# Segment loop of a recurrent-memory attention: smaller working tiles, 46 instead of 44 weight blocks resident in SBUF

## The chip, the cores and the metric

The kernel runs on one core of one Trainium2 chip. The metric is the device time of one execution in microseconds; of repeated executions the median counts. The engines are TensorE (PE in the profile), VectorE (DVE), ScalarE (ACT), GpSimd (POOL) and SyncE (SP); sixteen DMA engines move data between HBM and SBUF.

## What is computed

Two independent parts are computed and concatenated along the last axis. Part A is an attention with 32 heads of 128 over segments of 32 rows, with 8 memory rows that come from the segment before:

```python
mem = mem0                                  # 8 x 1024
for s in range(64):                         # 2048 rows in segments of 32
    h = concatenate([mem, x[32*s : 32*s+32]])        # 40 rows
    q, k, v = h @ Wq, h @ Wk, h @ Wv                 # 1024 -> 32 heads x 128 each
    p = softmax(where(mask, q @ k.T / sqrt(128), -1e9))
    o = (p @ v) @ Wo                                 # 4096 -> 1024
    mem = o[:8]                                      # into the next segment
    out_a[32*s : 32*s+32] = o[8:]
```

Since the memory of a segment is the output of the one before, the 64 segments run one after the other. The four weights have 4 million bf16 elements each, 32 MB together, which is more than SBUF holds. Part B is a state-space convolution of a 2048 x 1024 input with 128 complex modes per channel, done as a discrete Fourier transform with matmuls; the change does not touch it.

## The kernel before

**Order of the whole.** First part B is computed; in its shadow, on the same queues, everything of part A that doesn't depend on the memory is prepared (class `Ahead`, L60): the transposed x of each segment (`XTd`), and for the last 8 rows of each segment, which the code calls left rows, their projections k, q and v, packed as 768 columns per segment (`PKd`). Then comes the segment loop (L273 to L454), which is the subject here, and at the end an epilogue that projects the left rows' outputs of all segments with Wo at once (L458 on), from `OLd`. Inside the loop a segment therefore has 32 "main" rows in the projections: 24 rows of x and 8 memory rows. They sit in `hT`, [128, 8 chunks of 1024, 32 rows].

**Weights.** The weights are cut into 64 blocks of 128 x 2048 bf16 (512 KB, 4 KB per partition): for k, q and v each 2 halves t (16 heads) of 8 chunks kc of the contraction, and 16 units of Wo (two heads each). 44 blocks stay in SBUF for the whole loop (`W_res`). 20 are streamed in every segment from a DRAM copy: `STREAM` (L24) names the chunks kc of each projection and `STREAM_O` (L25) the units of Wo. `unit` (L223) returns the resident tile or issues a load on SP's queue into one of the four slots of `wst`. A load waits until the matmuls that use the slot's former block are done. The loop is written under a manual schedule: each engine executes its instructions in the order in which the code issues them, and waits come from data and from slots that are reused.

**A segment.** `quads` (L278) multiplies hT with the eight chunks of one half of a projection: per chunk four matmuls, 32 columns of the array each, that run beside each other, into one PSUM bank `acc`. `evac` copies it to SBUF as bf16 on ACT. `tr` (L295) transposes the 16 heads with TensorE into a PSUM tile, copied on DVE to KT or on ACT to QT. `scores` (L308) sets the mask with a matmul and adds q k^T for the main rows (index 0) and for the left rows (index 1), whose q is read from `pk`, into a PSUM tile `sc` of 8 x 40 columns. The keys are 32 main and 8 left ones. `softmax_a` (L321) takes the maximum, subtracts it in PSUM (DVE) and writes the exponential to an SBUF tile `ex` in bf16 (ACT). `softmax_b` (L329) sums and scales `ex` on DVE. `ptrans` (L336) transposes its 32 x 32 blocks on DVE into `pt` (main keys) and `pl` (left keys). `blocks` (L343) spreads them, multiplied by constant masks, to block-diagonal operands: `pb` and `lb` for the main queries on DVE, `pbl` and `lbl` for the left queries on POOL (`left_blocks`, L372). `pv` (L347) multiplies them with V. `oproj` (L378) multiplies the result oT with Wo, per unit eight matmuls, again four beside each other, into `po`.

The order in time is: k0, q0, k1, scores and softmax of half 0, q1, v0, scores and softmax of half 1, v1 (with pv of half 0 in its middle), projection units 0 to 7, pv of half 1, both pv of the left rows into `pvl`, units 8 to 15, then `osb` (L441), its transposition back into hT (`tro`, L448 and L449) and the stores. On POOL's queue lie the small loads and stores: `load_xt` one segment ahead, the copy into hT (`put_xt`), `load_pk`, the store of the left rows' oTL to `OLd` (L451) and four stores of osb (L454). `WARM` and `TAIL` are 0, so `warm` issues nothing; its PSUM tile still takes a bank.

PSUM's eight banks are divided in two for `acc`, two for `tr`, two for `att` (sc, pv, pvl), one for `warm` and one for `po`.

Of the kernel before, what the change touches and what calls it, by code (L numbers as in the profile page):

```python
# [23 lines left out]
STREAM = {("k", 0): (0, 4), ("q", 0): (0, 4), ("k", 1): (0, 4), ("q", 1): (0, 4), ("v", 0): (0, 4), ("v", 1): (0, 3, 6)}  # L24
STREAM_O = (0, 2, 5, 7, 9, 12, 14)  # L25
# [34 lines left out]
class Ahead:  # L60
# [34 lines left out]
    def projections(self, ps, tag):  # L95
# [11 lines left out]
        n = 0  # L107
        for i, (m, t, c) in enumerate(slices):
            w = ws[i]
            g, h2 = c // 2, 2 * (c % 2)  # L110
            mo = 0 if m == "k" else 256
            if m != "v" and c == 0:
                st = self.pool.tile([128, NS, 4, 4, XL], BF16, name="kst", tag="kst")
            for j in range(2):
# [26 lines left out]
                elif c == 7 and j == 1:  # L141
                    for r in range(8):
                        def put(r=r, mo=mo, t=t, st=st):
                            nc.sync.dma_start(out=PKd[8 * r:8 * r + 8, :, mo + 128 * t:mo + 128 * t + 128].rearrange("s p f -> p s f"),
                                              in_=st[:, 8 * r:8 * r + 8].rearrange("p s a b c -> p s (a b c)"))
                        late.append(put)
# [29 lines left out]
def part_a(ctx, tc, x, mem0, src, WD, HE, seg_len, out_a, ahead, W_res, rest):  # L176
# [12 lines left out]
    WARM = 0  # L189
    TAIL = 0  # L190
# [53 lines left out]
    ps_w = ctx_l.enter_context(tc.tile_pool(name="a_warm", bufs=1, space=PSUM))  # L244
    warm_ps = ps_w.tile([128, 512], F32, name="warm")
    warm_w = W_res["k", 0, 1]

    def warm(n):

        for _ in range(n):  # L250
            nc.tensor.matmul(warm_ps[:], lhsT=ident[:], rhs=warm_w[:, 0:512], start=True, stop=True, skip_group_check=True)
# [19 lines left out]
    xt = load_xt(1)  # L271
    pk = load_pk(0)
    for s in range(NS):  # L273
        vl = pk[:, 512:768].rearrange("p (t e) -> p t e", t=2)
        kl = pk[:, 0:256].rearrange("p (t a g k) -> p t a g k", t=2, a=4, g=4)
        ql = pk[:, 256:512].rearrange("p (t a g k) -> p t a g k", t=2, a=4, g=4)

        def quads(m, t, kcs, a=None):  # L278
            if a is None:
                a = ps_acc.tile([128, 512], F32, name="acc", tag="acc")  # L280
            for kc in kcs:
                w = unit((m, t, kc))
                if (m, t, kc) not in W_res:
                    warm(WARM)
# [18 lines left out]
        def new_kt(t):  # L303
            k = work.tile([128, 4, 4, NK], BF16, name="KT", tag="KT%d" % t)
            nc.gpsimd.tensor_copy(out=k[:, :, :, SL:NK], in_=kl[:, t])
            return k

        def scores(t, QT, KT):  # L308
# [6 lines left out]
            for hl in range(4):  # L315
                for g in range(4):
                    nc.tensor.matmul(sc[32 * g:32 * g + XL, 1, hl, :], lhsT=ql[:, t, hl, g, :], rhs=KT[:, hl, g, :],  # L317
                                     start=False, stop=True, tile_position=(0, 32 * g), skip_group_check=True)
            return sc[:].rearrange("p a b k -> p (a b) k")

        def softmax_a(sc):  # L321
# [3 lines left out]
            ex = work.tile([128, 8, NK], BF16, name="ex", tag="ex")  # L325
            nc.scalar.activation(out=ex[:], in_=sc, func=ACT.Exp, scale=scale)
            return ex

        def softmax_b(ex):  # L329
            ss = work.tile([128, 8], F32, name="ss", tag="ss")  # L330
            nc.vector.tensor_reduce(out=ss[:], in_=ex[:], axis=AX.X, op=ALU.add)
            rs = work.tile([128, 8], F32, name="rs", tag="rs")
            nc.vector.reciprocal(out=rs[:], in_=ss[:])
            nc.vector.tensor_tensor(out=ex[:], in0=ex[:], in1=bc(rs[:].unsqueeze(2), [128, 8, NK]), op=ALU.mult)

        def ptrans(t, ex):  # L336
            pt = work.tile([128, 8, 32], BF16, name="pt", tag="pt", bufs=2)
            nc.vector.transpose(out=pt[:], in_=ex[:, :, 0:SL])  # L338
            pl = work.tile([128, 2, 32], BF16, name="pl", tag="pl", bufs=2)
            nc.vector.transpose(out=pl[:], in_=ex[:, :, SL:NK])  # L340
            return pt, pl

        def blocks(eng, pt, pl, n, pb, lb):  # L343
            eng.tensor_tensor(out=pb, in0=bc(pt.unsqueeze(2), [128, 4, 4, n]), in1=bc(BD[:].unsqueeze(1).unsqueeze(3), [128, 4, 4, n]), op=ALU.mult)  # L344
            eng.tensor_tensor(out=lb, in0=bc(pl.unsqueeze(1), [128, 16, n]), in1=bc(BDL[:].rearrange("p a b -> p (a b)").unsqueeze(2), [128, 16, n]), op=ALU.mult)  # L345

        def pv(p, t, V, pb, lb):  # L347
            for hl in range(4):
                nc.tensor.matmul(p[:, hl, :], lhsT=V[:, 128 * hl:128 * hl + 128], rhs=pb[:, hl, :, :].rearrange("p a b -> p (a b)"),  # L349
                                 start=(hl == 0), stop=False, skip_group_check=True)  # L350
            nc.tensor.matmul(p.rearrange("p a b -> p (a b)"), lhsT=vl[:, t, :], rhs=lb.rearrange("p a b -> p (a b)"),  # L351
                             start=False, stop=True, skip_group_check=True)

        def new_qt(t):
            return work.tile([128, 4, 4, SL], BF16, name="QT", tag="QT%d" % t)

        def soft_blocks(t, ex):
            softmax_b(ex)
            pt, pl = ptrans(t, ex)
            pb = work.tile([128, 4, 4, SL], BF16, name="pb", tag="QT%d" % t)  # L360
            lb = work.tile([128, 16, SL], BF16, name="lb", tag="KT%d" % t)
# [789 lines left out]
```

## Time and profile before

| | |
|---|---|
| time, median of 3 runs | 3127.32 us (3118.98 to 3138.32) |
| the profiled execution's own time, its span | 3130.83 us, 3129.1 us |
| busy: PE, PEld, DVE, ACT, POOL | 70%, 36%, 42%, 31%, 25% of the span |
| HBM read, written | 809.26 MB, 68.42 MB |
| mean granted TensorE clock | 0.884 |
| share of SP's queue in the time of 16 DMA engines | 72.3% |

How to read it: the share of busy time is an average over part B (the first third), the loop (two thirds) and the epilogue, so the loop has to be looked at by itself. A busy TensorE is not TensorE at its peak, since the ends of matmuls are modelled. "Idle before" in a group of instructions is the time in which the engine waited, and the name behind it is what came last; idle time of an engine that is not the bound costs nothing. Times without unit in profile lines are us, durations of one instruction ns.

### The profile page before, as it was taken

What the parts mean: (1) busy time and instruction counts of PE and PEld (TensorE: products, weight loads), DVE (VectorE), ACT (ScalarE), POOL (GpSimd) and SP (SyncE); (2) the same over time, 40 slices, a digit from 0 to 9 for tenths busy, and PEclk for the clock granted to TensorE, in tenths of its full rate; (3) what the DMA queues carried; (4) which work ended last, traced back from release to release, by engine and by line L of the source; (5) the groups of instructions that cost most, each with busy time, mean ns of one, the idle gap of its engine ahead of it and who ended that gap; (6) DMA issues with size and microseconds to landing.
All of it is one profiled execution on the core that took longest, in us unless ns stands there. A gap on an engine that the chain in (4) does not pass through costs nothing.

```text
span 3129.1 us, 75740 instructions
## 1 busy us (share of the span) xinstructions
PE 2197.9 (70%) x32774; PEld 1139.2 (36%) x32774; DVE 1301.2 (42%) x2302; ACT 968.3 (31%) x1394; POOL 772.8 (25%) x1249
## 2 busy tenths in 40 slices
PE   1487778756975777777777777777677777777747
PEld 0255445522432333333333333333333333333323
DVE  7576777749851323232323232323332232323220
ACT  4776888611211222222222222212222222222210
POOL 2344344340001222222222222222222122222210
PEclk7699999868987898999998988889998899989878
DMA  4456653453358999999999999999999999999991
GB/s 119 134 156 187 189 150 104 126 159 104 122 198 314 352 348 351 349 350 351 352 342 337 351 344 348 333 346 332 347 356 341 331 353 345 342 355 346 347 330 56
DMA packets 394655, 868.02 MB, mean 277 GB/s; under 512 B 116726, under 2 KB 187382, under 8 KB 392272
## 3 DMA queue, kind: packets, MB, share of 16 engines
q1 hardware_dynamic: 353634, 789.62, 72.3%
q0 software_dynamic: 24912, 51.52, 5.0%
q10 hardware_dynamic: 15774, 22.03, 2.2%
q8 instruction: 256, 4.19, 0.5%
q14 instruction: 79, 0.65, 0.1%
HBM read 809.26 MB, written 68.42 MB: 280 GB/s over the span
## 4 chain that ended last, share of the span: by engine, by line
DMA 52%; PE 21%; issue 13%; ACT 5%; DVE 4%; POOL 4%; SPq 1%; ACTq 0%; POOLq 0%; DVEq 0%
DMA wst<-WD_o 17%; DMA wst<-WD_q 15%; DMA wst<-WD_v 11%; PE acc L286 8%; DMA wst<-WD_k 5%; PE po L386 4%; PE pe L480 2%; DMA olr<-OLd 1%; ACT sn L863 1%; PE pro L125 1%; POOL us L747 1%; POOL us L748 1%; PE pv L349 1%; DMA PVd<-vst 1%; PE ups L742 1%
## 5 line engine op out<-in xcount | busy, mean ns | idle before, releaser
L286 PEld LDWEIGHTS <-hT 128*32 128x32 bf16 x12288 | 317.1, 99 | 646.5 <-issue 338.4
L286 PE MATMUL acc<-wst,hT 128*32 128x512 bf16 x3328 | 348.9, 405 | 279.7 <-DMA wst<-WD_k 113.7
L292 ACT CAST qk<-acc 128x512 bf16<-128x512 f32 x256 | 149.8, 585 | 763.0 <-PE acc L286 762.0
L386 PEld LDWEIGHTS <-oT 128*32 128x32 bf16 x8192 | 243.1, 109 | 375.6 <-issue 303.2
L386 PE MATMUL po<-wst,oT 128*32 128x256 bf16 x3584 | 213.3, 321 | 236.9 <-DMA wst<-WD_o 234.1
L344 POOL TENSOR_TENSOR pbl<-pt,BD 128x128 bf16<-128x128 bf16 x128 | 91.3, 713 | 822.4 <-DVE pt L338 818.1
L298 DVE COPY KT<-tr 128x512 bf16<-128x512 bf16 x128 | 54.4, 425 | 569.9 <-PE tr L297 569.9
L441 DVE CAST osb<-po 128x256 bf16<-128x256 f32 x64 | 27.2, 425 | 584.6 <-PE po L386 584.6
L386 PE MATMUL po<-W_o,oT 128*32 128x256 bf16 x4608 | 250.0, 318 | 22.4 <-ACT oT L369 22.4
L286 PE MATMUL acc<-W_q,hT 128*32 128x512 bf16 x3072 | 231.2, 406 | 0.0
L286 PE MATMUL acc<-W_k,hT 128*32 128x512 bf16 x3072 | 231.1, 408 | 0.0
L286 PE MATMUL acc<-W_v,hT 128*32 128x512 bf16 x2816 | 211.3, 383 | 0.0
L369 ACT CAST oT<-pv 128x512 bf16<-128x512 f32 x128 | 74.8, 585 | 435.7 <-PE pv L351 435.7
L454 POOL DMA_DIRECT2D out_dram<-osb x256 | 129.2, 512 | 198.6 <-DVE osb L441 187.8
L1037 PE MATMUL yp<-Bt,mi 128*128 128x512 bf16 x384 | 116.8, 413 | 34.7 <-DVE Bt L991 17.1
L323 DVE TENSOR_REDUCE mx<-sc 128x8 f32<-128x320 f32 x128 | 62.3, 487 | 187.3 <-PE sc L317 187.2
L955 PE MATMUL hps<-KT,MF 128*128 128x512 bf16 x384 | 100.2, 410 | 51.9 <-DVE x L966 29.0
L298 ACT COPY QT<-tr 128x512 bf16<-128x512 bf16 x128 | 74.9, 585 | 151.9 <-PE tr L297 145.6
L125 PE MATMUL pro<-xTl,wsl 128*128 128x512 bf16 x512 | 115.1, 380 | 7.6 <-DVE ua L744 4.6
L345 DVE TENSOR_TENSOR lb<-pl,BDL 128x512 bf16<-128x512 bf16 x128 | 119.4, 933 | 0.0
L256 POOL DMA_DIRECT2D pk<-PKd x64 | 37.5, 586 | 325.1 <-PE pvl L351 316.5
L839 DVE SCALAR_TENSOR_TENSOR nr<-kM,ptt 128x656 f32<-128x656 f32 x128 | 106.1, 829 | 20.6 <-ACT kM L838 20.5
(259 smaller groups left out, 3876.8 us busy)
## 6 DMA issues: line engine op xcount, KB each, us to landing
wst<-WD_o SPq DMA_DIRECT2D x448, 512.0 KB, 5.7
wst<-WD_v SPq DMA_DIRECT2D x320, 512.0 KB, 5.4
wst<-WD_k SPq DMA_DIRECT2D x256, 512.0 KB, 5.6
wst<-WD_q SPq DMA_DIRECT2D x256, 512.0 KB
Ud<-ux POOLq DMA_DIRECT2D x16, 1024.0 KB, 5.5
uq<-Ud SPq DMA_DIRECT2D x32, 512.0 KB, 5.1
pk<-PKd POOLq DMA_DIRECT2D x64, 192.0 KB, 5.3
wsl<-in_A_Wk_dram SPq DMA_DIRECT2D x16, 512.0 KB, 5.4
```

Source lines behind the costliest of these rows:

```text
L125: nc.tensor.matmul(a[:], lhsT=w[:, kc, 128 * j:128 * j + 128], rhs=xTl[:, kc, :, :].rearrange("p s k -> p (s k)"), start=(kc == 0), stop=( ...
L286: nc.tensor.matmul(a[32 * g:32 * g + 32, :], lhsT=hT[:, kc, :], rhs=w[:, 512 * g:512 * g + 512], start=(kc == 0), stop=(kc == KC - 1), til ...
L292: nc.scalar.copy(out=q[:], in_=a[:])
L298: eng(out=dst, in_=p[:, i, :, :, :])
L344: eng.tensor_tensor(out=pb, in0=bc(pt.unsqueeze(2), [128, 4, 4, n]), in1=bc(BD[:].unsqueeze(1).unsqueeze(3), [128, 4, 4, n]), op=ALU.mult)
L345: eng.tensor_tensor(out=lb, in0=bc(pl.unsqueeze(1), [128, 16, n]), in1=bc(BDL[:].rearrange("p a b -> p (a b)").unsqueeze(2), [128, 16, n]) ...
L369: nc.scalar.copy(out=o[:], in_=p[:].rearrange("p a (g q) -> p a g q", g=4))
L386: nc.tensor.matmul(po[32 * qt:32 * qt + 32, :], lhsT=oT[:, h % 4, (h % 16) // 4, :], rhs=w[:, 1024 * hh + 256 * qt:1024 * hh + 256 * qt + ...
L454: nc.gpsimd.dma_start(out=out_a[r0:r0 + XM, 256 * qt:256 * qt + 256], in_=osb[32 * qt:32 * qt + XM, :])
L839: v.scalar_tensor_tensor(out=nrs[e // 4][:, e % 4].rearrange("p f t j -> p f (t j)"), in0=kM[:], scalar=MAGIC, in1=ptv, op0=ALU.subtract, ...
L955: pe.matmul(ps[:], lhsT=MF[:, 4 * rr + mc, cs, 128 * kc:128 * kc + 128], rhs=rhs, start=(i == 0 and mc == 0), stop=(i == 1 and mc == 3))
L1037: pe.matmul(yp[:], lhsT=m_[:, cs, kc, :], rhs=Bt[:, kc, half, j, c_, :], start=(n == 0), stop=(n == 15))
```

## The change

Two more of the weight blocks stay in SBUF (46), and 18 are streamed: chunks 0 and 4 of every projection half (v1 had 0, 3 and 6), and units 0, 3, 5, 8, 11 and 13 of Wo (before 0, 2, 5, 7, 9, 12 and 14). The room comes from the loop's working tiles:

- The softmax stays in its PSUM tile: the exponential is written back to `sc` in f32, sum, reciprocal (both in the tile `mx`) and scaling work there, and the 32 x 32 transposes go from PSUM to a PSUM tile `pt` in f32, which takes the bank of `warm`. `warm` is gone.
- Tiles share single slots by lifetime: A holds k0, k1, V0 and o0; B holds q0, q1, pb0 and o1; C holds KT0, KT1 and lb1; E holds QT0, QT1, V1 and `ob` (osb and oTL in one tile); F holds xt and the second half of lb0; L holds the left rows' blocks. The first half of lb0, and later pb1, are written into the part of `pk` whose k and q have been used; to that end `pk` has its columns in another order (k and q of half 0, then of half 1).
- The left rows' blocks are made on DVE (`spread`, `spread_l`), and lb0 in two halves.
- The load of xt is issued in the segment before, behind the first pv, and no longer one segment ahead of that. The pv of the left rows of half 0 follows the first pv, and `pvl` and `po` share one PSUM bank `pp`; oTL is copied at the end, behind osb.

The diff, without the changed PKd columns in `Ahead` (L111, L143 to L145) and the removal of `warm`:

```diff
-STREAM = {..., ("v", 0): (0, 4), ("v", 1): (0, 3, 6)}
-STREAM_O = (0, 2, 5, 7, 9, 12, 14)
+STREAM = {..., ("v", 0): (0, 4), ("v", 1): (0, 4)}
+STREAM_O = (0, 3, 5, 8, 11, 13)
...
-        xt = pers.tile([128, KC, XM], BF16, name="xt", tag="xt")
+        xt = work.tile([128, KC, XM], BF16, name="xt", tag="F")
...
         def evac(a, tag):
-            q = work.tile([128, 512], BF16, name=tag, tag=tag, bufs=2 if tag == "qk" else 1)
+            q = work.tile([128, 512], BF16, name="ev", tag=tag)
...
         def softmax_a(sc):
             mx = work.tile([128, 8], F32, name="mx", tag="mx")
             nc.vector.tensor_reduce(out=mx[:], in_=sc, axis=AX.X, op=ALU.max)
             nc.vector.tensor_tensor(out=sc, in0=sc, in1=bc(mx[:].unsqueeze(2), [128, 8, NK]), op=ALU.subtract)
-            ex = work.tile([128, 8, NK], BF16, name="ex", tag="ex")
-            nc.scalar.activation(out=ex[:], in_=sc, func=ACT.Exp, scale=scale)
-            return ex
+            nc.scalar.activation(out=sc, in_=sc, func=ACT.Exp, scale=scale)
+            return mx, sc
...
+        def softmax_b(mx, ex):
+            nc.vector.tensor_reduce(out=mx[:], in_=ex, axis=AX.X, op=ALU.add)
+            nc.vector.reciprocal(out=mx[:], in_=mx[:])
+            nc.vector.tensor_tensor(out=ex, in0=ex, in1=bc(mx[:].unsqueeze(2), [128, 8, NK]), op=ALU.mult)
+            pt = ps_s.tile([128, 10, 32], F32, name="pt", tag="pt")
+            nc.vector.transpose(out=pt[:, 0:8, :], in_=ex[:, :, 0:SL])
+            nc.vector.transpose(out=pt[:, 8:10, :], in_=ex[:, :, SL:NK])
+            return pt[:, 0:8, :], pt[:, 8:10, :]
+        def spread(out, pt, n):
+            nc.vector.tensor_tensor(out=out, in0=bc(pt.unsqueeze(2), [128, 4, 4, n]), in1=bc(BD[:].unsqueeze(1).unsqueeze(3), [128, 4, 4, n]), op=ALU.mult)
+        def spread_l(out, pl, j, m, n):
+            nc.vector.tensor_tensor(out=out, in0=bc(pl.unsqueeze(1), [128, m, n]),
+                                    in1=bc(BDL[:].rearrange("p a b -> p (a b)")[:, j:j + m].unsqueeze(2), [128, m, n]), op=ALU.mult)
+        def left_blocks(S):
+            L = work.tile([128, 2, 16, XL], BF16, name="L", tag="L")
+            spread(L[:, 0].rearrange("p (a b) k -> p a b k", a=4), S[0][:, 4:8, 0:XL], XL)
+            spread_l(L[:, 1], S[1][:, 1, 0:XL], 0, 16, XL)
+            return L
...
+        sc0 = scores(0, QT0, KT0)
+        st0, ex0 = softmax_a(sc0)
+        a = quads("q", 1, range(KC))
+        q1 = evac(a, "B")
         KT1 = new_kt(1)
-        sc0 = scores(0, QT0, KT0)
-        ex0 = softmax_a(sc0)
-        a = quads("q", 1, range(KC))
-        q1 = evac(a, "qk")
         p1 = new_tr()
         tr(p1, 0, k1, KT1[:, :, :, 0:SL])
-        S0 = soft_blocks(0, ex0)
+        S0 = softmax_b(st0, ex0)
         a = quads("v", 0, H0)
-        QT1 = new_qt(1)
+        QT1 = new_qt()
         tr(p1, 1, q1, QT1[:], nc.scalar.copy)
+        lb0a = pk[:, 0:256]
+        lb0b = work.tile([128, 256], BF16, name="lb0b", tag="F")
+        spread_l(lb0a..., S0[1][:, 0, :], 0, 8, SL)
+        spread_l(lb0b[:]..., S0[1][:, 0, :], 8, 8, SL)
+        pb0 = work.tile([128, 4, 4, SL], BF16, name="pb0", tag="B")
+        spread(pb0[:], S0[0][:, 0:4, :], SL)
+        L0 = left_blocks(S0)
         quads("v", 0, H1, a)
-        V0 = evac(a, "V0")
+        V0 = evac(a, "A")
         sc1 = scores(1, QT1, KT1)
-        ex1 = softmax_a(sc1)
-        L0 = left_blocks(0, S0)
+        st1, ex1 = softmax_a(sc1)
         a = quads("v", 1, H0)
-        o0 = pv_x(0, S0, V0)
+        pv0 = pv_x(0, V0, pb0..., [lb0a, lb0b[:]], "A")
+        pp = ps_o.tile([128, 2, 256], F32, name="pp", tag="pp")
+        pl_ = pp[:, 0, :].rearrange("p (t a k) -> p t a k", t=2, a=4)
+        pv_l(pl_, 0, V0, L0)
+        o0 = evac_o(pv0, "A")
+        if s + 1 < NS:
+            xt = load_xt(s + 1)
         quads("v", 1, H1, a)
-        V1 = evac(a, "V1")
+        V1 = evac(a, "E")
         if s + 1 < NS:
             put_xt(xt)
-            if s + 2 < NS:
-                xt = load_xt(s + 2)
-        S1 = soft_blocks(1, ex1)
-        L1 = left_blocks(1, S1)
+        S1 = softmax_b(st1, ex1)
+        pb1 = pk[:, 0:512].rearrange("p (a b k) -> p a b k", a=4, b=4)
+        spread(pb1, S1[0][:, 0:4, :], SL)
+        lb1 = work.tile([128, 16, SL], BF16, name="lb1", tag="C")
+        spread_l(lb1[:], S1[1][:, 0, :], 0, 16, SL)
+        L1 = left_blocks(S1)
...
-        oproj(po, range(0, 8), o0)
-        o1 = pv_x(1, S1, V1)
-        pl_ = ps_att.tile([128, 2, 4, 32], F32, name="pvl", tag="att")
-        pv(pl_[:, 0], 0, V0, L0[0][:], L0[1][:])
-        pv(pl_[:, 1], 1, V1, L1[0][:], L1[1][:])
+        oproj(pp[:, 1, :], range(0, 8), o0)
+        pv1 = pv_x(1, V1, pk..., [lb1...], "B")
+        o1 = evac_o(pv1, "B")
+        pv_l(pl_, 1, V1, L1)
         if s + 1 < NS:
             pk = load_pk(s + 1)
...
+        ob = work.tile([128, 2, 256], BF16, name="ob", tag="E")
+        osb = ob[:, 0, :]
+        nc.vector.tensor_copy(out=osb, in_=pp[:, 1, :])
+        nc.scalar.copy(out=ob[:, 1, :], in_=pp[:, 0, :])
```

More of the change, by code (lines that the diff above doesn't have):

```diff
@@ L303, in new_kt @@
         def new_kt(t):
[L304 to L305 removed]
+            k = work.tile([128, 4, 4, NK], BF16, name="KT", tag="C")
+            nc.gpsimd.tensor_copy(out=k[:, :, :, SL:NK], in_=kl[t])
             return k
@@ L336, in ptrans @@
[L336 to L345, printed above, removed]
@@ new lines, in pv @@
+        def pv(p, t, V, pb, lbs, first=True):
+            for hl in range(4):
+                nc.tensor.matmul(p[:, hl, :], lhsT=V[:, 128 * hl:128 * hl + 128], rhs=pb[:, hl, :],
+                                 start=(first and hl == 0), stop=False, skip_group_check=True)
+            n = 4 // len(lbs)
+            for i, lb in enumerate(lbs):
+                nc.tensor.matmul(p[:, n * i:n * i + n, :].rearrange("p a b -> p (a b)"), lhsT=vl[:, t, :], rhs=lb,
+                                 start=False, stop=True, skip_group_check=True)
@@ L370, in pv_x, with pv_l @@
             return o
-        def left_blocks(t, S):
-            pbl = work.tile([128, 4, 4, XL], BF16, name="pbl", tag="pbl%d" % t)
-            lbl = work.tile([128, 16, XL], BF16, name="lbl", tag="lbl%d" % t)
-            blocks(nc.gpsimd, S[0][:, 4:8, 0:XL], S[1][:, 1, 0:XL], XL, pbl[:], lbl[:])
-            return pbl, lbl
+        def pv_l(pl_, t, V, L):
+            pv(pl_[:, t], t, V, L[:, 0].rearrange("p (a b) k -> p a (b k)", a=4), [L[:, 1].rearrange("p a k -> p (a k)")], first=(t == 0))
@@ L449, in part_a @@
             nc.vector.tensor_copy(out=hT[:, :, XM:SL].rearrange("p (q j) r -> p j q r", j=2), in_=pt_o[:, :, :, XM:SL])
-            warm(TAIL)
-        nc.gpsimd.dma_start(out=OLd[s], in_=oTL[:].rearrange("p t a b -> p (t a b)"))
+        nc.gpsimd.dma_start(out=OLd[s], in_=ob[:, 1, :])
         r0 = s * SL
```

79 lines of the change are left out of this document (24 added, 55 removed).

## The prediction

> **What bounds the kernel now.** I read the head of the page and its chain of waits first, then the stamps of one instruction that runs once per segment, then the windows of the steady loop, then what TensorE waits for in it.
>
> ```profile
> span 3129.1 us, 75740 instructions
> ...
> DMA 52%; PE 21%; issue 13%; ACT 5%; DVE 4%; POOL 4%; SPq 1%; ACTq 0%; POOLq 0%; DVEq 0%
> DMA wst<-WD_o 17%; DMA wst<-WD_q 15%; DMA wst<-WD_v 11%; PE acc L286 8%; DMA wst<-WD_k 5%; PE po L386 4%; PE pe L480 2%; DMA olr<-OLd 1%; ACT sn L863 1%; PE pro L125 1%; POOL us L747 1%; POOL us L748 1%; PE pv L349 1%; DMA PVd<-vst 1%; PE ups L742 1%
> ```
>
> The four streamed kinds of weight block make up 48% of the whole chain. The instruction that copies a segment's result out of PSUM dates the loop:
>
> ```profile
> L441 DVE CAST osb<-po x64: 423/425/426, 1035.7 to 3023.3; 128x256 bf16<-128x256 f32 x64
> ```
>
> 63 periods in 1987.6 us: **31.55 us per segment**. Ahead of it and behind it lie 1035.7 and 105.8 us. Next the windows (stretch, its length, busy time of PE, PEld, DVE, ACT and POOL, granted clock, DMA share, GB/s), the loop's middle first, and parts of one segment after it:
>
> ```profile
> 1200.00:2800.00 1600.00, 1166.68 (x21486) 584.09 (x21486) 494.50 (x1119) 354.77 (x661) 371.89 (x707) 0.91 0.96 345
> 1989.00:1997.00 8.00, 6.33 (x154) 2.92 (x146) 5.08 (x12) 3.21 (x6) 1.70 (x2) 1.00 0.86 280
> 1997.00:2015.00 18.00, 11.25 (x206) 6.62 (x210) 3.96 (x10) 2.47 (x5) 5.72 (x12) 0.89 0.99 361
> 2015.00:2025.00 10.00, 9.27 (x156) 4.03 (x145) 1.42 (x3) 2.87 (x6) 0.00 (x0) 0.85 0.94 319
> 2000.00:2004.00 4.00, 1.88 (x48) 1.15 (x41) 1.01 (x2) 0.71 (x2) 2.06 (x4) 1.00 0.94 334
> 2004.00:2008.00 4.00, 3.14 (x43) 1.88 (x46) 0.00 (x0) 0.72 (x2) 0.09 (x1) 0.57 1.02 346
> ```
>
> DMA is the bound, but not everywhere: from v1 through the output projection to the next segment's first blocks the queue is full at 361 GB/s; where k1, q1 and v0 run, TensorE is busy 79 to 93% of the time and the rate falls to 280 to 319. The four wst slots do not smooth that out. TensorE's waits in the same 1600 us (total, times, longest):
>
> ```profile
> PE po L386 <- DMA wst<-WD_o: 190.0, 233, 2.7
> PE acc L286 <- DMA wst<-WD_v: 65.0, 101, 2.8
> PE acc L286 <- DMA wst<-WD_k: 63.8, 69, 2.6
> PE acc L286 <- DMA wst<-WD_q: 53.9, 105, 1.9
> PE tro L448 <- DVE osb L441: 26.7, 50, 0.5
> ```
>
> The four DMA rows sum to 372.7 us, times 31.55/1600 = **7.35 us of waiting for weights per segment**. So a segment costs TensorE 31.55 - 7.35 = **24.2 us** without such waits. That is the other floor.
>
> **What two blocks less are worth.** DMAs of the loop, same stretch:
>
> ```profile
> wst<-WD_o SPq DMA_DIRECT2D x357, 512.0 KB, 5.7
> wst<-WD_v SPq DMA_DIRECT2D x254, 512.0 KB, 5.4
> wst<-WD_k SPq DMA_DIRECT2D x201, 512.0 KB, 5.7
> wst<-WD_q SPq DMA_DIRECT2D x200, 512.0 KB
> pk<-PKd POOLq DMA_DIRECT2D x51, 192.0 KB, 5.3
> OLd<-oTL POOLq DMA_DIRECT2D x50, 64.0 KB, 5.2
> out_dram<-osb POOLq DMA_DIRECT2D x200, 12.0 KB, 5.2
> xt<-XTd POOLq DMA_DIRECT2D x51, 48.0 KB, 5.1
> ```
>
> Per segment 20 x 512 + 192 + 64 + 4 x 12 + 48 = 10,592 KB = 10.85 MB, which over 31.55 us is 344 GB/s: the window's 345, so nothing else of weight moves. With 18 blocks it is 9,568 KB = 9.80 MB. At the same mean rate 9.80/10.85 x 31.55 = **28.5 us**, 3.05 us less; that still leaves TensorE 4.3 us of waiting.
>
> I do not take all of it. The blocks go where the queue is full (one from v1, one from the output projection), and TensorE's share of the period rises from 24.2/31.55 = 77% to 85%, so the stretch at 280 to 319 GB/s grows: v1 now has four chunks of matmuls per streamed block, as k1, q1 and v0 have. Today: some 9 us at 300 GB/s (2.7 MB) and 22.5 us at 360 (8.1 MB), together 10.8 MB. If the dense stretch stays 9 us, 7.1 MB remain at 360: 9 + 19.7 = 28.7 us. If it grows to 12 us, 6.2 MB remain: 12 + 17.2 = 29.2 us. I take the middle, **28.95 us**: 2.6 us less per segment, x 63 = 164 us.
>
> Outside the loop: two more residents are loaded ahead of it (1 MB, 3 us at 345 GB/s), the first segment streams two blocks less (the same 3 us): nothing net. Two DRAM copies less lie in part B, off the loop. The epilogue is unchanged; which slots its loads wait for can move by a few us either way.
>
> **What may eat it.** *Softmax in place.* Rows of DVE for the old forms (busy, mean ns, idle before):
>
> ```profile
> L345 DVE TENSOR_TENSOR lb<-pl,BDL 128x512 bf16<-128x512 bf16 x102 | 95.1, 933 | 0.0
> L344 DVE TENSOR_TENSOR pb<-pt,BD 128x512 bf16<-128x512 bf16 x102 | 69.6, 682 | 0.0
> L324 DVE TENSOR_TENSOR sc<-sc,mx 128x320 f32<-128x320 f32 x102 | 51.0, 500 | 7.1
> L334 DVE TENSOR_TENSOR ex<-ex,rs 128x320 bf16<-128x320 bf16 x102 | 50.5, 495 | 3.5
> L323 DVE TENSOR_REDUCE mx<-sc 128x8 f32<-128x320 f32 x102 | 49.6, 487 | 150.3 <-PE sc L317 150.3
> L331 DVE TENSOR_REDUCE ss<-ex 128x8 f32<-128x320 bf16 x102 | 49.1, 481 | 28.7 <-ACT ex L326 28.7
> L338 DVE STREAM_TRANSPOSE pt<-ex 128x256 bf16<-128x256 bf16 x102 | 45.4, 445 | 7.1
> ```
>
> L324 (f32 in PSUM, in place) against L334 (bf16 in SBUF), and L323 against L331, differ by 1%: sum and scaling move to PSUM for nothing. The Trainium skill (VectorE: DVE Perf Modes, "Rules for kernel authors") says the opposite: accept the single rate on PSUM operands, or copy to SBUF first where many operations follow, since a 16-bit tensor_tensor in SBUF runs at twice the rate. By that rule scaling would lose about half a microsecond; the pair L324/L334 shows no such gap, and the row decides.
>
> No row shows a 32x32 transpose of f32 in PSUM: 0.45 us like L338 (I take this, by the two pairs above), 0.89 us if it goes by bytes; it could gain nothing worth counting. Spreading from f32: L344's 0.68, up to 0.80 by L324's rate (500 x 512/320). The left blocks, 2 x 128 elements per half on DVE, cost 0.5 us at a third of L344 each, between 0.35 (a quarter of L344 each, by element) and 0.9 (two of L338, which has twice the elements). The third spread instruction (lb0 in halves) costs 0.2, what an instruction on 8 elements takes:
>
> ```profile
> L333 DVE RECIPROCAL rs<-ss 128x8 f32<-128x8 f32 x102 | 20.7, 203 | 3.5
> ```
>
> POOL's work beside DVE disappears, and L345's 933 should come down to the undisturbed 690:
>
> ```profile
> 2000.33 0.69 DVE L345 TENSOR_TENSOR lb<-pl,BDL 128x512 bf16<-128x512 bf16 x1
> ```
>
> DVE per half: +0.5 - 0.25, at the high end +2.0. DVE is busy 494.50/1600 x 31.55 = 9.8 us per segment: 10.5 to 14 after it, no bound. The path is what counts. This spread ends the second softmax, at 2001.02; its scores ended at 1996.26 and its reader starts at 2006.15:
>
> ```profile
> 1995.99 0.27 PE L317 MATMUL sc<-KT,pk 128*8 128x40 bf16 x16
> 2006.15 0.61 PE L349 MATMUL pv<-pb,V 128*128 128x128 bf16 x4
> ```
>
> That is 5.1 us of slack, given by v1, the first eight units of the output projection and their weight waits; with fewer waits some 3 us remain, and the lateness is 0.3 to 2 us. Hidden; uncovered it costs 0.3 to 2 us x 63 = 20 to 126 us.
>
> *Slots shared by lifetime.* DVE now waits, ahead of pb0, for the transposes of q1 (slot B); behind it queue L0 and the second softmax, and their readers come a v0 half later: covered. POOL's KT1 copy waits for the first scores; nobody needs it before p1. The xt load leaves its place one segment ahead: POOL issues it after the first pv, the copy into hT and then the pk load queue behind it.
>
> ```profile
> 1999.07 0.38 PE L351 MATMUL pv<-lb,pk 128*128 128x512 bf16 x1
> ```
>
> From 1999.45 it lands in 5.1 us, at about 2005; the segment ends at 2011.69 (the store rows below), and only the next one reads hT: covered. The pk load, which waits for the second pv (2006.15) anyway, loses nothing. The tight one is slot E: the copy of QT0 on ACT now waits until the previous segment's output DMAs have landed, and the k1 evacuation queues behind it.
>
> ```profile
> 2011.69 2.02 POOL L454 DMA_DIRECT2D out_dram<-osb  x4 [2.66 <-DVE osb L441]
> 2020.60 0.59 ACT L298 COPY QT<-tr 128x512 bf16<-128x512 bf16 x1 [0.99 <-PE tr L297]
> DMA to landing us min/median/max: 2.0/5.1/8.4
> ```
>
> The last of the four is issued at 2013.2 and lands at 2018.3, at worst 2021.6: 2.3 us early to 1.0 us late. Up to 1 us per segment at the worst; I take nothing, since the five blocks ahead of that copy stay.
>
> **Sum**, against the profiled execution's own 3130.83 us (span 3129.1, 1.7 around it): 3130.8 - 164 = 2967. It lay 3.5 above the median of the runs, 3127.32, so **2963 us**.
>
> **Rivals.**
> *The whole saving* (2935 us): the rate stays 345 GB/s or rises, 28.5 us per segment, 63 x 3.05 = 192. For it: the loop's stretches run at 361. A clock effect would bring it: 2000:2004 has TensorE busy for 47% at clock 1.00, and the next 4 us run at 0.57; shorter waits would mean fewer such dips and less than 24.2 us of TensorE time, down to 22 at the extreme (24.2 x 0.91). The Trainium skill (TensorE: Matmul & The Clock Gate, "The HAM clock gate") states such a rule: a window of about 3.4 us with little activity halves the clock; the two rows agree. With that even 28.0 us, so 2903, is thinkable. 22%.
> *A latency chain takes over* (about 3030): waits shorten, but the softmax path (2 us) and slot E (1 us) come out uncovered beside 24.2 of TensorE, with about 3 us of waits left: 30.2 us per segment, 85 us saved, 3042 from the profile, 3038 from the median. For it: 4.3 us of remaining wait is little cover. Against: stalls below the four slots' depth are caught up. 16%.
> *Nothing gained* (3127): if slot turnaround rather than bytes sets the pace, fewer blocks bring nothing. Against it are 7.35 us of waits named for these very blocks. 4%.
> *Slower* (3160 and up): the in-place softmax on DVE becomes the chain. Each half is followed by its reader with some 3 us of slack; TensorE must lose all 7.35 us of today's waits and 0.5 more for a loss of 1%. That takes some 5 to 7 us more per half, where my high end is 2.0; PSUM transposes and spreads at 3 to 4 times their rows. No row of an f32 PSUM operation points there. 4%.
>
> **Chances.** Forecast (28.6 to 29.4 us, 2941 to 2992) 54%. One per cent, about what a measurement tells from no change, is 31 us, or 0.5 us per segment. Faster 0.92, same 0.04, slower 0.04. Range: 2915 (28.2 us) to 3040, which takes in most of the whole saving and the chain's case.
>
> **What would show it.** wst DMAs 18 per segment and the osb stamps 28.6 to 29.4 us apart; mean rate 335 to 345 GB/s; WD waits of TensorE down from 7.35 to some 4 us, most of the loss in the WD_o row; pt transposes near 450 ns; no pbl on POOL. The forecast is wrong if TensorE waits for DVE's pb or ACT's QT for over 1 us per segment, if transposes take over 1 us, or if the rate falls below 325 GB/s.

## The result and the profile after

The changed kernel takes **2946.5 us** (median, 2942.2 to 2955.9), the kernel before 3126.0 us in the same measurement: a ratio of 0.943 (95% interval 0.939 to 0.947). The prediction was 2963 us, with a range from 2915 to 3040. The profiled execution took 2950.68 us.

The head of the changed kernel's page and its chain of waits:

```profile
span 2949.0 us, 75939 instructions
...
DMA 43%; PE 20%; issue 20%; DVE 6%; ACT 6%; POOL 5%; SPq 0%; ACTq 0%; POOLq 0%; DVEq 0%
DMA wst<-WD_o 14%; DMA wst<-WD_v 9%; PE acc L273 9%; DMA wst<-WD_k 8%; DMA wst<-WD_q 7%; PE pp L371 2%; PE pe L476 2%; DMA olr<-OLd 1%; ACT sn L859 1%; PE pro L125 1%; POOL us L743 1%; POOL us L744 1%; ACT oT L358 1%; PE tr L284 1%; PE ups L738 1%
```

The streamed blocks are 38% of the chain, against 48% before. The stamps of the copy of a segment's result (the line's first and last start), the loop's middle by windows, and what TensorE waits for in those 1600 us:

```profile
L440 DVE CAST ob<-pp x64: 424/425/426, 1026.5 to 2842.2; 128x256 bf16<-128x256 f32 x64
```

```profile
1200.00:2800.00 1600.00, 1220.41 (x23566) 629.63 (x23558) 582.95 (x1490) 386.68 (x722) 257.56 (x557) 0.93 0.96 342
```

```profile
PE pp L371 <- DMA wst<-WD_o: 154.6, 197, 3.2
PE acc L273 <- DMA wst<-WD_k: 46.6, 74, 1.8
PE acc L273 <- DMA wst<-WD_q: 44.3, 98, 1.9
PE acc L273 <- DMA wst<-WD_v: 40.8, 54, 1.8
```

A segment takes 1815.7/63 = **28.82 us** instead of 31.55, which is 172 of the 180 us between the two profiled spans. The waits for weights sum to 286.3 us in 1600, or 5.16 us per segment (7.35 before), so TensorE without them needs 23.7 us (24.2 before). The row of WD_o shrinks most, from 3.75 to 2.78 us per segment, but that is 0.97 of the 2.19 us lost and not most of it. The mean rate of the DMA queue is the same as before to 1%: 342 GB/s. The other 8 us lie ahead of the loop, whose first stamp is 9 us earlier; between the runs below that stamp lies anywhere from 1026 to 1043 us (1002 only where nothing is streamed), without following the number of residents, so this is not counted as an effect of the change.

The new forms on DVE, in the same stretch:

```profile
L321 DVE STREAM_TRANSPOSE pt<-sc 128x256 f32<-128x256 f32 x110 | 51.2, 465 | 3.8
...
L330 DVE TENSOR_TENSOR lb<-pt,BDL 128x512 bf16<-128x512 f32 x55 | 37.5, 681 | 0.0
L327 DVE TENSOR_TENSOR L<-pt,BD 128x128 bf16<-128x128 f32 x110 | 30.9, 281 | 0.0
```

A transpose of f32 within PSUM takes 465 ns, against 445 for bf16 in SBUF; the spread `lb` comes down from 933 to 681 ns; an instruction for a left block takes 281 ns.

### The profile page after: what moved, and what is told of

It reads as the page before. It is cut to its first block, busy times and chain, and to the rows that moved or that the text cites. A ratio compares the mean times of both kernels' runs of the same rounds, so it can differ in the third digit from the quotient of the medians.

```text
span 2949.0 us, 75939 instructions
## 1 busy us (share of the span) xinstructions
PE 2124.8 (72%) x32791; PEld 1128.5 (38%) x32838; DVE 1355.8 (46%) x2622; ACT 967.4 (33%) x1394; POOL 599.2 (20%) x993
## 4 chain that ended last, share of the span: by engine, by line
DMA 43%; PE 20%; issue 20%; DVE 6%; ACT 6%; POOL 5%; SPq 0%; ACTq 0%; POOLq 0%; DVEq 0%
DMA wst<-WD_o 14%; DMA wst<-WD_v 9%; PE acc L273 9%; DMA wst<-WD_k 8%; DMA wst<-WD_q 7%; PE pp L371 2%; PE pe L476 2%; DMA olr<-OLd 1%; ACT sn L859 1%; PE pro L125 1%; POOL us L743 1%; POOL us L744 1%; ACT oT L358 1%; PE tr L284 1%; PE ups L738 1%
## 5 line engine op out<-in xcount | busy, mean ns | idle before, releaser
L273 PE MATMUL acc<-wst,hT 128*32 128x512 bf16 x3072 | 330.2, 415 | 203.2 <-DMA wst<-WD_k 85.2
L279 ACT CAST ev<-acc 128x512 bf16<-128x512 f32 x384 | 225.4, 587 | 528.5 <-PE acc L273 485.8
L371 PE MATMUL pp<-wst,oT 128*32 128x256 bf16 x3072 | 167.0, 296 | 215.8 <-DMA wst<-WD_o 180.7
L273 PE MATMUL acc<-W_k,hT 128*32 128x512 bf16 x3072 | 249.7, 434 | 0.0
L371 PE MATMUL pp<-W_o,oT 128*32 128x256 bf16 x5120 | 231.5, 294 | 0.0
L440 DVE CAST ob<-pp 128x256 bf16<-128x256 f32 x64 | 27.2, 425 | 369.7 <-issue 365.2
L252 POOL DMA_DIRECT2D xt<-XTd x64 | 35.9, 561 | 483.9 <-PE pp L345 395.8
L292 POOL COPY KT<-pk 128x128 bf16<-128x128 bf16 x128 | 38.4, 300 | 462.3 <-PE sc L304 449.4
L450 POOL DMA_DIRECT2D out_dram<-ob x256 | 129.7, 513 | 6.0 <-issue 5.9
L313 ACT ACTIVATE sc<-sc 128x320 f32<-128x320 f32 x128 | 54.0, 422 | 189.0 <-DVE sc L312 157.0
```

Source lines behind the costliest of these rows:

```text
L273: nc.tensor.matmul(a[32 * g:32 * g + 32, :], lhsT=hT[:, kc, :], rhs=w[:, 512 * g:512 * g + 512], start=(kc == 0), stop=(kc == KC - 1), til ...
L371: nc.tensor.matmul(po[32 * qt:32 * qt + 32, :], lhsT=oT[:, h % 4, (h % 16) // 4, :], rhs=w[:, 1024 * hh + 256 * qt:1024 * hh + 256 * qt + ...
L450: nc.gpsimd.dma_start(out=out_a[r0:r0 + XM, 256 * qt:256 * qt + 256], in_=osb[32 * qt:32 * qt + XM, :])
```

## The experiments

Two theories went into the first runs: A, that of the prediction, and that the other edits of the change are worth something of their own (B gain, C loss).

**The change without the two blocks.** The changed kernel with the streamed sets of before:

```diff
-..., ("v", 1): (0, 4)}
-STREAM_O = (0, 3, 5, 8, 11, 13)
+..., ("v", 1): (0, 3, 6)}
+STREAM_O = (0, 2, 5, 7, 9, 12, 14)
```

> The changed kernel with the streamed sets of before (20 blocks streamed, 44 resident): everything of the change except the two blocks. Theory A, the one of the prediction (the stream of weight blocks sets the pace, the other edits hide in its waits): a segment of 31.3 to 31.8 us as before, 3110 to 3140 us in all. Rival B (the restructured softmax, shorter queues and slots are worth something by themselves): below 3095 us. Rival C (they cost something that the two blocks outweigh): above 3150 us.

Measured: 3136.6 us, 1.004 of before (1.002 to 1.007). Stamps (first and last start of the copy, as above):

```profile
L440 DVE CAST ob<-pp x64: 424/425/426, 1040.2 to 3024.7; 128x256 bf16<-128x256 f32 x64
```

That is 31.50 us per segment, as before (31.55). Softmax in PSUM, shared slots, left blocks on DVE, the later xt load: all of it together changes the segment by 0.05 us. In the profiled execution the 0.4% do not lie in the segments; its first stamp comes 4.5 us later than before.

**The two blocks without the change.** The kernel before with the streamed sets of after, and

```diff
+ALIAS = {("v", 1, 3): ("v", 1, 2), ("o", 2): ("o", 1)}
     def unit(key):
+        key = ALIAS.get(key, key)
```

> The kernel before with the streamed sets of after (18 blocks). Since 46 residents don't fit into its SBUF, two blocks (chunk 3 of v1 and unit 2 of Wo) are not loaded at all: their matmuls read the resident chunk 2 of v1 and unit 1 of Wo, so the output isn't the reference's; all matmuls are there. Theory A: the same segment as in the changed kernel, 28.6 to 29.1 us, 2935 to 2970 us in all (up to 6 us less than the changed kernel, since two residents less are loaded ahead of the loop). Rival B: above 2990. Rival C: below 2925.

Measured: 2949.2 us, 0.942 of before (0.938 to 0.946), the changed kernel's time. Its stamps:

```profile
L444 DVE CAST osb<-po x64: 424/425/426, 1030.5 to 2848.0; 128x256 bf16<-128x256 f32 x64
```

28.85 us per segment. The two runs together show that the number of streamed blocks is the whole effect on the period, and B and C fall. The other edits are hidden, though, and not free. Waits for weights taken off, TensorE needs 24.2 us per segment in the kernel before and 24.8 with the edits at 20 blocks, 23.1 and 23.7 at 18 blocks: the edits cost it 0.6 us at either count, 0.4 us of that in waits for other engines. The waits for weights are shorter by as much (7.35 against 6.72 us, 5.77 against 5.16), so the period stays. This is what a loop shows whose pace is set by its weight loads.

**One block at a time.** The changed kernel with the third block of v1, and with the seventh of Wo.

> The changed kernel with 19 blocks streamed: v1 with three (chunks 0, 3 and 6), Wo with six. Theory A (bytes): half of the two blocks' worth, 1.37 us per segment, so 86 us more than the changed kernel, 3020 to 3045 us. Rival D (what a block is worth depends on where it is streamed; the queue is full during the output projection and has slack where TensorE is dense): a block in v1 costs under 60 us, below 3005 us.

> The changed kernel with 19 blocks streamed: v1 with two, Wo with seven (units 0, 2, 5, 7, 9, 12, 14). Theory A (bytes): 3020 to 3045 us, within 10 us of the run with the third block in v1. Rival D (position): above 3055 us.

Measured: 3053.1 us with the block in v1 (0.976, 0.973 to 0.980), 3036.6 us with the block in Wo (0.972, 0.969 to 0.974). Stamps of the first and of the second:

```profile
L440 DVE CAST ob<-pp x64: 423/425/426, 1041.7 to 2949.2; 128x256 bf16<-128x256 f32 x64
```

```profile
L440 DVE CAST ob<-pp x64: 424/425/426, 1029.8 to 2923.4; 128x256 bf16<-128x256 f32 x64
```

In the loop, where it counts, 30.28 and 30.06 us per segment: 1.46 and 1.24 us more than the changed kernel, together 2.70, which is what both cost (31.50 - 28.82 = 2.68). The blocks are additive and nearly equal. D falls too: a block where TensorE is dense is not cheaper. The run with the block in v1 lies 8 us above its expected range and 17 us above the other, where A had said at most 10. The two profiled executions lie 25 us apart, 63 x 0.22 = 14 us of it in the segments and 12 us ahead of the loop; with one profile of each, the 0.2 us by which a block in v1 seems to cost more is not settled.

**Is there slack on the softmax path?** Three more spread instructions per half:

```diff
         L0 = left_blocks(S0)
+        for _ in range(3):
+            spread(pb0[:], S0[0][:, 0:4, :], SL)
...
         L1 = left_blocks(S1)
+        for _ in range(3):
+            spread_l(lb1[:], S1[1][:, 0, :], 0, 16, SL)
```

> The changed kernel with three more spread instructions per half on DVE, right before their reader: pb0 written three more times behind L0, lb1 three more times behind L1 (same values; 3 x 0.68 us = 2.04 us per half on the softmax path, 4.1 us of DVE per segment). Theory A: some 3 us of slack per half hide it, at most 0.3 us per segment more, 2935 to 2965 us. Rival (the softmax path is the next chain and already close): 1 us or more per segment uncovered, above 3010 us.

Measured: 3098.2 us, 0.991 of before (0.987 to 0.995): 152 us more than the changed kernel. Stamps, and what TensorE waits for in 1200 us:

```profile
L444 DVE CAST ob<-pp x64: 423/425/425, 1043.3 to 3003.1; 128x256 bf16<-128x256 f32 x64
```

```profile
PE pv L345 <- DVE lb L330: 90.0, 38, 2.6
PE pv L341 <- DVE pb L327: 72.0, 38, 2.7
```

31.11 us per segment, 2.29 more, out of 4.1 us that were added. The 3 us of slack per half are not there; the rival is right. The two rows are 4.2 us of waiting per segment, and the waits for weights fall from 5.2 to 2.6 us beside them: what covered the softmax path was the waits for weights. The changed kernel's own trace has the real slack. These are the last left blocks of half 0 and of half 1 on DVE:

```profile
2050.30 0.28 DVE L330 TENSOR_TENSOR L<-pt,BDL 128x128 bf16<-128x128 f32 x1
...
2055.66 0.28 DVE L330 TENSOR_TENSOR L<-pt,BDL 128x128 bf16<-128x128 f32 x1
```

And these are the first matmuls of the two pv, which read pb0 and pb1 (the left blocks have their readers behind them, at 2051.60 and 2057.47):

```profile
2051.15 0.40 PE L341 MATMUL pv<-pb,ev 128*128 128x128 bf16 x4
...
2057.02 0.40 PE L341 MATMUL pv<-pk,ev 128*128 128x128 bf16 x4
```

DVE is done with everything 0.6 and 1.1 us ahead of these matmuls; by what pv needs of it, pb0 (ended 2050.18) and lb1 (ended 2055.54), it is 1.0 and 1.5 us. This segment is no outlier: between 1300 and 2000 us the medians of the latter two are about 0.8 and 1.0 us.

**More slots.** The changed kernel with six slots for its 18 blocks, two residents not loaded:

```diff
-    wst = ctx_w.enter_context(tc.tile_pool(name="a_wst", bufs=4, side="right"))
+    wst = ctx_w.enter_context(tc.tile_pool(name="a_wst", bufs=6, side="right"))
+ALIAS = {("k", 0, 1): ("k", 0, 2), ("q", 0, 1): ("q", 0, 2)}
```

> The changed kernel with six slots for streamed blocks instead of four, still 18 streamed. The room comes from two residents that are not loaded (chunk 1 of k0 and of q0; their matmuls read chunk 2, so the output isn't the reference's). Theory A as the prediction has it (four slots don't smooth out the dense stretch, and the rate falls there): 27.3 to 28.2 us per segment at 350 GB/s or more, 2850 to 2905 us. Rival E (the mean rate of about 344 GB/s is what the queue gives, whatever the slots): 28.5 us or more per segment, above 2925 us.

Measured: 2695.7 us, 0.861 of before (0.858 to 0.865), 154 us below the expected range of A and 229 below E's bound. Stamps, windows, and the time from issue to landing of the streamed blocks:

```profile
L443 DVE CAST ob<-pp x64: 423/424/426, 1026.2 to 2587.2; 128x256 bf16<-128x256 f32 x64
```

```profile
1200.00:2400.00 1200.00, 987.13 (x20588) 527.69 (x20577) 509.17 (x1304) 331.52 (x631) 223.63 (x485) 1.00 1.02 398
```

```profile
DMA to landing us min/median/max: 5.0/7.2/8.5
```

24.78 us per segment at 398 GB/s and clock 1.00. The same queue that gave 342 to 346 GB/s with four slots and 18 to 20 blocks (317 in the run with more spreads) gives 398 with six. E falls, and A is right only in its direction: it took four slots to lose a little in the dense stretch, while they hold the whole rate down. This became theory F: the number of slots, that is of loads in flight, sets the rate, and the 344 GB/s belong to four.

**How far down it goes.** 16 blocks, and none at all:

```diff
-..., ("v", 1): (0, 4)}
-STREAM_O = (0, 3, 5, 8, 11, 13)
+..., ("v", 1): (0,)}
+STREAM_O = (0, 3, 7, 10, 13)
+ALIAS = {("v", 1, 4): ("v", 1, 3), ("o", 5): ("o", 6)}
```

```diff
-STREAM = {...}
-STREAM_O = (0, 3, 5, 8, 11, 13)
+STREAM = {}
+STREAM_O = ()
+ALIAS = {**{(m, t, kc): (m, t, kc + 1) for m in "kqv" for t in range(2) for kc in (0, 4)}, **{("o", u): ("o", u + 1) for u in (0, 3, 5, 8, 11, 13)}}
```

> The changed kernel with 16 blocks streamed: chunk 4 of v1 and unit 5 of Wo are not loaded, their matmuls read the resident chunk 3 of v1 and unit 6 of Wo (the output isn't the reference's). Theory A: 8.75 MB per segment at 342 GB/s, 25.6 us, some coupling added 25.6 to 26.2, 2745 to 2785 us. Rival (a chain of TensorE, DVE and ACT near 28 us takes over right below the present point): 26.8 us or more, above 2820 us.

> The changed kernel without any streaming: the 18 streamed blocks are neither copied nor loaded, their matmuls read the resident block behind each (the output isn't the reference's). What is left is the floor of TensorE with the latencies between the engines. Theory A: 22 to 24.5 us per segment (31.55 - 7.35 = 24.2 before, 28.82 - 5.16 = 23.7 after, less if the clock stays at 1.00), 2510 to 2675 us. Rival (the waits for weights hide other waits, which come out): 25.5 us or more, above 2735 us.

Measured: 2788.8 us (0.890, 0.885 to 0.894) and 2528.4 us (0.808, 0.803 to 0.812). Stamps:

```profile
L443 DVE CAST ob<-pp x64: 423/424/426, 1032.5 to 2691.7; 128x256 bf16<-128x256 f32 x64
```

```profile
L443 DVE CAST ob<-pp x64: 423/424/425, 1002.3 to 2421.3; 128x256 bf16<-128x256 f32 x64
```

That is 26.34 and 22.52 us per segment. 16 blocks miss A's range by 4 us and stay 31 us below the rival's bound: two blocks fewer give 2.48 us where the step from 20 to 18 gave 2.68. Without streaming, TensorE and the latencies between the engines take 22.5 us, so the changed kernel still has 6.3 us above that floor.

**Residents traded for slots.** F says that a slot is worth more than a resident block. Three kernels that compute everything, the first two from the changed kernel, the third from the kernel before:

```diff
 20 blocks (sets of before), 44 residents
-bufs=4
+bufs=6
 19 blocks (Wo units 0, 2, 5, 7, 9, 12, 14), 45 residents
-bufs=4
+bufs=5
 kernel before, 21 blocks (Wo units 0, 2, 4, 6, 8, 10, 12, 14), 43 residents
-bufs=4
+bufs=5
```

> The changed kernel with 44 residents, 20 streamed blocks (the sets of before) and six slots: the room of the two freed residents spent on slots. Computes everything. Theory F (four slots cap the queue at about 344 GB/s, six reach 398 as in the run with six slots): 10.85 MB per segment at 390 to 400 GB/s, 27.1 to 27.8 us, 2835 to 2885 us. Theory A as the prediction had it (a byte streamed costs 1/344 us per KB whatever the slots, six slots helped only because 18 blocks left little to wait for): 30 us or more per segment, above 3020 us.

> The changed kernel with 45 residents, 19 streamed blocks (v1 two, Wo seven) and five slots. Computes everything. Theory F: a rate midway between 344 and 398, some 371 GB/s: 10.32 MB in 27.8 us, 27.3 to 28.4 us, 2850 to 2920 us. Theory A: the 30.06 us of 19 blocks with four slots, less little, above 3000 us.

> The kernel before, nothing of the change, with one resident block given up for a fifth slot: 43 residents, 21 streamed (Wo units 0, 2, 4, 6, 8, 10, 12, 14), five slots. Computes everything. Theory F: 11.37 MB per segment at the 383 GB/s that five slots gave in the changed kernel, 29.7 us instead of 31.55, so 3005 to 3035 us, faster than before although a block more is streamed. Theory A (the mean rate of 344 GB/s belongs to the queue): 33 us per segment, above 3195 us.

Measured: 2861.0 us (0.916, 0.912 to 0.921), 2848.4 us (0.912, 0.907 to 0.916) and 2970.9 us (0.950, 0.946 to 0.954). All three are far from A. The first two beat both kernels of the case, with more bytes streamed than in the changed kernel. They are also the cleanest test of the slots, since each differs from a run above in the number of slots alone: 31.50 us per segment with 20 blocks and four slots become 27.31 with six, and 30.06 with 19 blocks (the third of them in Wo) become 27.14 with five. F had the first within its range; the second is 2 us faster than F's range, at 383 GB/s where 371 were expected. The third reaches most of the change's gain from the kernel before by one line and one set, at 21 blocks per segment; it is 34 us faster than F expected, since its rate is 392 GB/s and not 383, and why is open. Stamps of the one with six slots (27.31 us per segment), then stamps and windows of the two with five (27.14 and 29.07 us):

```profile
L440 DVE CAST ob<-pp x64: 424/424/426, 1029.8 to 2750.2; 128x256 bf16<-128x256 f32 x64
```

```profile
L440 DVE CAST ob<-pp x64: 424/424/425, 1033.6 to 2743.3; 128x256 bf16<-128x256 f32 x64
```

```profile
1200.00:2600.00 1400.00, 1110.08 (x21952) 574.03 (x21948) 545.97 (x1398) 355.39 (x674) 235.80 (x513) 0.96 1.00 383
```

```profile
L441 DVE CAST osb<-po x64: 424/425/425, 1030.2 to 2861.6; 128x256 bf16<-128x256 f32 x64
```

```profile
1200.00:2600.00 1400.00, 1075.88 (x20334) 537.95 (x20328) 464.23 (x1056) 332.71 (x624) 372.98 (x672) 0.93 1.01 392
```

**Smaller slots.** The changed kernel with each streamed block loaded in halves into eight half slots:

```diff
-        t_ = wst.tile([128, 2048], BF16, name="wst", tag="w")
-        nc.sync.dma_start(out=t_[:], in_=WD[key][:])
+        for i in range(2):
+            t_ = wst.tile([128, 1024], BF16, name="wst", tag="w")
+            nc.sync.dma_start(out=t_[:], in_=WD[key][:, 1024 * i:1024 * i + 1024])
```

> The changed kernel with its 18 streamed blocks loaded as two halves of 1024 columns (256 KB, rows of 2 KB) into eight slots of half the size: same room, same bytes, 36 loads per segment. Computes everything. Theory F: what counts is the bytes in flight, and half of a block that is being used is free earlier; 27.0 to 28.8 us per segment, 2830 to 2945 us. Rival (each load has a fixed turn-around that now comes twice as often, or the shorter rows slow the queue): 29.3 us or more, above 2975 us.

Measured: 2944.5 us, 0.944 of before (0.939 to 0.949): no difference from the changed kernel, 28.83 us per segment at 342 GB/s. Stamps:

```profile
L443 DVE CAST ob<-pp x64: 424/424/426, 1037.4 to 2853.8; 128x256 bf16<-128x256 f32 x64
```

Twice the loads cost nothing, and the finer release, from which F expected something, brings nothing. That fits the bytes in flight as what counts: 36 loads of 5.3 us (the landing time of the halves) in 28.83 us are 6.6 half blocks under way, or 3.3 whole ones, against 3.5 in the changed kernel.

## Why the prediction was right, and where not

**The number.** 28.95 us per segment were predicted and 28.82 measured, 164 us in the loop against 172. The part-by-part claim that nothing but the two blocks has a price came out (31.50 us for the change with 20 blocks, 28.85 for the old kernel with 18).

**The step that was wrong is the first: "DMA is the bound", with 361 GB/s as a full queue.** I took the rate as a property of the queue and the falls to 280 to 319 as what the slots lose. The runs put it in another way. Landing time is the time from a load's issue until its data are there. The blocks in flight, on average, are the blocks per segment times the median landing time over the period. The changed kernel's landing time in the loop, as one of the rows that the table is made of:

```profile
DMA to landing us min/median/max: 4.3/5.6/7.1
```

| run | blocks | slots | us per segment | GB/s | landing, us | in flight |
|---|---|---|---|---|---|---|
| before | 20 | 4 | 31.55 | 345 | 5.5 | 3.5 |
| after | 18 | 4 | 28.82 | 342 | 5.6 | 3.5 |
| after, 20 blocks | 20 | 4 | 31.50 | 346 | 5.4 | 3.4 |
| after, 19 blocks (Wo) | 19 | 4 | 30.06 | 346 | 5.5 | 3.5 |
| after, 19 blocks (Wo) | 19 | 5 | 27.14 | 383 | 6.2 | 4.3 |
| before, 21 blocks | 21 | 5 | 29.07 | 392 | 6.3 | 4.6 |
| after, 20 blocks | 20 | 6 | 27.31 | 399 | 7.3 | 5.3 |
| after, 18 blocks | 18 | 6 | 24.78 | 398 | 7.2 | 5.2 |

With four slots some 3.5 blocks are under way on average: seven eighths of a slot's time is the flight of its block, and only half a slot's worth is spent on matmuls and on issuing. That by itself shows no bound, since five and six slots are as full (86 to 91% in all rows). What shows it is that one more slot with 19 blocks shortens the period by 2.9 us, and two more with 20 blocks by 4.2 us, with nothing else changed. The loop is bound by the turn-around of four slots, 4 x 31.55/20 = 6.3 us before and 4 x 28.82/18 = 6.4 us after. Two blocks fewer are two turns fewer, 2 x 6.3/4 = 3.15 us, which is nearly what they are as bytes at 344 GB/s (3.05 us): both counts give the same answer as long as the number of slots stays, and so the prediction came out right with the wrong owner of the rate. That was luck: the change happened to leave the number of slots alone. From four to five slots the rate grows by 11 to 14%, from five to six by 2 to 4%, while the landing time grows by 0.7 and then by 1 us: the queue's own limit seems to come near, though no run has more than six slots.

The Trainium skill (DMA: Bandwidth & Descriptors, "Measured") gives up to 425 GB/s for one core by itself with large transfers, measured on loads that GpSimd issues, and says that batches of 1 MiB or more are needed for three quarters of the peak. The 398 GB/s of six slots, on SP's queue, do not contradict the first. The second does not hold here, where several loads are under way: 512 KB blocks reach 398 GB/s, and 256 KB blocks the same 342 as 512 KB blocks in the same bytes of slots. In these runs the rate goes with the bytes in flight and not with the size of one transfer.

**The dense stretch.** "v1 has four chunks per block, the stretch grows": the loss against a constant rate was put at 0.45 us, and is 0.3 (28.82 against 28.5). The reason given for it is not borne out: if the block of v1 were the one that makes the stretch grow, giving it up would have been worth less than the block of Wo, and the runs with one block point the other way, if anywhere (1.46 against 1.24 us). Where the 0.3 us come from is not shown.

**Softmax in place.** Prices per instruction were right: the transposes 465 ns for 450, the spread 681 for 690, two left blocks 0.56 us for 0.5. Scaling takes 499 ns in PSUM and 495 in SBUF, as the pair L324/L334 said. The rule of the Trainium skill (VectorE: DVE Perf Modes, "Rules for kernel authors") is not refuted by that: it promises the double rate for bf16 operands with step 1, and in L334 the second operand `rs` is f32, eight elements read over 40 columns each. The cover was wrong: "some 3 us remain" per half, and the medians of the changed kernel are about 0.8 and 1.0 us. I had read the slack off half 1 alone, behind which the output projection's weight waits stand, and had taken off too little of them. Half 0 had 2.7 us in the same segment of the kernel before:

```profile
1995.24 0.89 DVE L345 TENSOR_TENSOR lb<-pl,BDL 128x512 bf16<-128x512 bf16 x1
```

```profile
1998.83 0.40 PE L349 MATMUL pv<-pb,V 128*128 128x128 bf16 x4
```

Over the segments between 1300 and 2000 us, its median there is 1.3 us and that of half 1 is 4.0. With the edits alone half 1 has 3.8 us, with the two blocks alone 1.8 us: the blocks take most of the slack, the edits less. The edits add 0.4 us of DVE per half (9.8 us busy per segment before, 10.5 after), and that still fits; the run with three more spreads shows that 2 us more per half, my high end, would have cost most of the gain.

**Slots by lifetime.** The tight one was named (E), and taken at nothing. In the changed kernel ACT waited for the stores in 7 of the 56 segments of the stretch, and TensorE for QT 3 times:

```profile
ACT QT L285 <- DMA out_dram<-ob: 18.2, 7, 4.5
```

```profile
PE sc L300 <- ACT QT L285: 5.9, 3, 2.6
```

5.9 us of TensorE in 1600, or 0.1 us per segment, within the bound of 1 us. With six slots and shorter segments it is 25.0 us in 1200, five times as much per segment, and ACT waits for the stores in 28 of 48 segments:

```profile
PE sc L303 <- ACT QT L288: 25.0, 33, 3.2
```

**The clock.** The rival that hangs on it did happen in part: the granted clock in the loop rose from 0.91 to 0.93, TensorE's own time fell from 24.2 to 23.7 us (by 1.1 us with the blocks, less the 0.6 us of the edits), and waits of 5.2 us remain where "some 4" were predicted. With six slots and 18 blocks, where waits for weights are down to 1.2 us per segment, the clock is 1.00 in the windows row. The 22.5 us floor of the run without streaming is at clock 1.00 as well. The Trainium skill (TensorE: Matmul & The Clock Gate, "The HAM clock gate") says that the clock is halved after an idle window of about 3.4 us and full after a busy one. The order of the runs agrees; but in the kernel before TensorE never waited longer than 2.8 us for weights in the 1600 us, and the clock was 0.57 right after a stretch in which it was busy for 47%, so here less than an idle window was enough.

**The other rivals.** The latency chain did not take over at 18 blocks, but it is near: TensorE's waits for other engines than the DMA are 1.6 us per segment in the changed kernel and 3.0 us with six slots. In that rival's sum, 85 us off 3130.8 are 3046 from the profile and 3042 from the median, not 3042 and 3038, so the upper end of the range, 3040, just missed the case that it was to take in. "Nothing gained" was put at 4% with "slot turnaround rather than bytes sets the pace" as its reason, and that was bad reasoning: turn-around does set the pace, and each block is one turn.

**Open.** The start of the loop varies by up to 17 us between profiled runs, and what sets it was not looked into. Seven and more slots were not tried, nor a version that combines five slots with other places of the 19 blocks.

## What to carry to other kernels

A DMA share of 96% and a constant mean rate do not show that the queue is the bound. Multiply the transfers per period by their time to landing and divide by the period; when that comes out near the number of buffers, the buffers are hardly ever empty, and one more of them has to be tried. The count alone does not tell whether the buffers bind or the queue, since it was as near with six slots as with four, though the fifth slot raised the rate by 11 to 14% and the sixth by only 2 to 4%. Here a fifth slot was worth more than the block that its room could keep resident (19 blocks through five slots: 2848 us, 18 through four: 2946 us). When a change moves only a count, check that two readings of the bound (bytes and turns) give different numbers before taking one of them as shown. Slack read from a trace has to be read without the waits that the change removes, and for every place at which it is needed.

## What the hardware showed that was not expected

The landing time of a 512 KB load grows by only 0.7 to 1 us for each further slot (5.5, 6.2, 7.2 us with four, five and six), so that the rate still rises from 345 to 398 GB/s while the profile already calls the DMA engines 96% busy. Loads of half the size in twice as many slots moved the same 342 GB/s with a landing time of 5.3 us, nearly that of the whole blocks.
